# Sliding-window attention into a soft mixture of experts: the first pair of heads loaded as fp32 on another queue, q transposed later in each slot, the mixture's steps a slot later

## The chip, the cores and the metric

The kernel runs on one core of a Trainium2 chip. The core has five engines that work side by side, each with its own instruction queue: TensorE (PE, matmuls; PEld is its weight load), VectorE (DVE), ScalarE (ACT), GpSimd (POOL) and SyncE (SP). DMA transfers are issued from POOL's or SP's queue and run on 16 DMA engines. The metric is the device time of one execution in microseconds (us); lower is better.

## The reference

q, k and v are fp32 of batch 8, heads 8, sequence 576, head size 64. phi is 512 x 32; w1 and w2 hold 8 experts of 512 x 1024 and 1024 x 512.

```
scores = scale * q @ k^T, only where 0 <= row - column < 64
attn   = softmax(scores);  x = attn @ v, laid out as (8*576) x 512
logits = x @ phi
d = softmax of logits over the 4608 rows;  slot_input = d^T @ x   (32 slots, 4 for each expert)
slot_out = relu(slot_input @ w1[e]) @ w2[e]   for each expert
c = softmax of logits over the 32 slots;   out = c @ slot_out
```

## The kernel before

The work is cut into 32 pairs of heads, four pairs to a batch entry. The main loop (L461 to L546) has one slot for each n = 0 to 31, and each slot works on several pairs at different stages. The order of instructions on each engine is the order in which the code is written; each engine takes its queue strictly in turn.

**Loading.** `load_qk` issues from POOL the transfers of q and k for four heads, which turn fp32 into fp16 on the way; `load_v` does it for v and `load_w` for the experts' weights. `join(p)` copies one pair's q and k on POOL into `qi` and `ki`, heads interleaved, for slot p. The first pair's halves are loaded by `load_qk(0, ((0, 2),))`, before anything else on POOL.

**One slot.** PE transposes k (`turn`, into the PSUM tile `kb`) and q (into `qb`); ACT copies them out as `kT` (`keep_k`) and, in two halves, as `qz` (`keep_q`, L258). Scores of the pair three slots back follow: `score_last` into the rest of `kb`, `score_main` into `sc`; `lh` and `rt` add mask and row maximum as a bias. ACT takes the exponentials (`keep_last`, `keep_main`, L308). `st_turn` transposes the attention output x_b of the pair five slots back into the PSUM tile `tx`, and DVE copies it to `xt` (L350). `st_mask` (L265, L266) writes the window mask into the PSUM tile `mx`, on which `st_max` (L275) adds the scores of the pair before; DVE takes the row maximum (`keep_max`, L280). `st_shift` (L284) transposes the maxima, DVE casts them into `rt` (`keep_shift`, L287). `st_av` (L320) multiplies attention by v, `st_norm` normalises on DVE (L329, L330).

**Banks.** `kb`, `qb`, `tx`, the logits `lg` and the slot sums `si` share a ring of two PSUM banks: each new tile takes the bank of the tile before last and waits until that has been read. `mx`, `sc` and `av` are single tiles of their own.

**The mixture's steps.** From n = 8 on, each batch entry's steps are spread over four slots, fi = 0 to 3: the logits (`fr_logits`, `keep_logits`), their running maximum (`fr_max`) and their transposes (`fr_turned`) with the subtraction on POOL (`fr_combine_a`, L405); the exponential (`fr_exp`, L375) and its sums on POOL (`fr_stat`); the transposed dispatch weights (`turn_dispatch`, `keep_dispatch`), the slot sums (`fr_slots`, accumulated on DVE in L446) and the combine weights (`fr_combine_b` on ACT, `fr_combine_c` on DVE, `fr_place` on POOL). After the loop comes a tail: the last pairs, the experts, and the output, which SP's queue writes.

**Constants.** POOL builds the window mask `wb`, the score bias `mb` and `db` (L156 to L170) ahead of the loop; `constants(2)`, in slot 2, copies the bias into `lh` and `rt` on ACT and DVE. DVE's memsets of `kT`, `qz`, `v`'s columns of ones and others precede the loop too.

Of the kernel before, what the change touches and what calls it, by code (L numbers as in the profile page):

```python
# [20 lines left out]
def kernel(  # L21
# [65 lines left out]
    def load_qk(k_, parts=((0, 4),)):  # L87
        b, o = k_ // 2, 4 * (k_ % 2)
        if k_ not in staged:
            staged[k_] = (pin.tile([GP, 4, RQ * Dh], FP16, name="qs", tag="qs"),  # L90
                          pin.tile([GP, 4, RQ * Dh], FP16, name="ks", tag="ks"))
        for h0, h1 in parts:
            for t_, src in reversed(tuple(zip(staged[k_], (q, k)))):
                nc.gpsimd.dma_start(out=t_[:, h0:h1, :],
                                    in_=src[b, o + h0:o + h1].rearrange("h (p r) d -> p h (r d)", r=RQ))
# [34 lines left out]
    load_qk(0, ((0, 2),))  # L130
# [3 lines left out]
    load_qk(0, ((2, 4),))  # L134

# [6 lines left out]
    for t_ in kTs:  # L142
        nc.vector.memset(t_[:, 0:64], 0.0)
    for t_ in qzs:
        nc.vector.memset(t_, 0.0)
# [8 lines left out]
    join(0)  # L154
    load_qk(1)
    mb = ctr[0:64, 96:224]  # L156
    nc.gpsimd.memset(mb, 0.0)
    nc.gpsimd.affine_select(out=mb[:, 0:64], in_=mb[:, 0:64], compare_op=ALU.is_gt,
                            fill=NEG, base=0, pattern=[[1, 64]], channel_multiplier=-1)
    nc.gpsimd.affine_select(out=mb[:, 64:128], in_=mb[:, 64:128], compare_op=ALU.is_ge,  # L160
                            fill=NEG, base=0, pattern=[[-1, 64]], channel_multiplier=1)
    KR = 74
    db = ctr[0:KR, 224:235]
    nc.gpsimd.memset(db[64:KR, :], 0.0)
    nc.gpsimd.affine_select(out=db[64:KR, 0:9], in_=db[64:KR, 0:9], compare_op=ALU.not_equal, fill=-1.0,
                            base=0, pattern=[[-1, 9]], channel_multiplier=1)
    nc.gpsimd.affine_select(out=db[64:KR, 9:10], in_=db[64:KR, 9:10], compare_op=ALU.not_equal, fill=NEG,
                            base=-9, pattern=[[0, 1]], channel_multiplier=1)
    nc.gpsimd.affine_select(out=db[64:KR, 10:11], in_=db[64:KR, 10:11], compare_op=ALU.not_equal, fill=1.0,
                            base=-9, pattern=[[0, 1]], channel_multiplier=1)  # L170

    NR = 2
    ms = [const.tile([128, 33], FP16, name=f"m{i}") for i in range(2)]
    for t_ in ms:
        nc.vector.memset(t_[:, 10:33], 0.0)
    rts = [const.tile([128, 128], FP16, name=f"rt{i}") for i in range(NR)]
# [15 lines left out]
    wm = const.tile([128, 6, 96], FP16, name="wm")  # L192
    for t in range(2):
        nc.vector.tensor_copy(out=wm[64 * t:64 * t + 64],
                              in_=wb[:, :].unsqueeze(1).broadcast_to([64, 6, 96]))
    nc.vector.memset(wm[0:64, 0, 0:64], NEG)
    nc.vector.memset(wm[64:128, 0, 0:32], NEG)
# [8 lines left out]
    def constants(part):  # L206
        if part == 2:
# [28 lines left out]
    for _ in range(2):  # L236
        wp = bank([128, 512], FP32, "wp")
        for _ in range(4):
            nc.tensor.matmul(wp[:, :], warm[:, 0:128], warm[:, :], start=True, stop=True)

    av = pav.tile([128, 2, 512], FP32, name="av", tag="av")
    nc.vector.memset(av[64:128, :, 260:325], 1.0)
    mx = pmx.tile([128, 2, 512], FP32, name="mx", tag="mx")
    nc.vector.memset(mx[:, 1, 384:480], 0.0)

    xbs, pts, xts = {}, {}, {}
# [214 lines left out]
    for n in range(NP):  # L461
        b, hp = divmod(n, HP)
        constants(n)
# [44 lines left out]
        if fi == 3:  # L508
            turn(sides[n][0], qb)
            keep_q(n, qb)  # L510
# [5 lines left out]
        if fi == 1:  # L516
            fr_exp(fb)
        elif fi == 2:
            fr_combine_b(fb)
# [4 lines left out]
        if fi == 0:  # L524
            lg = bank([128, 192], FP32, "lg")
            fr_logits(fb, lg)
            keep_logits(lg, nc.vector.tensor_copy)
        elif fi == 2:
            fr_slots(fb, bank([128, D], FP32, "si"))
        elif fi == 3:  # L530
            fr_place(fb)
        if n >= 1:
            keep_max(n - 1)
        if fi == 0:
            fr_max(fb)
            fr_turned(fb, lgs)
            fr_combine_a(fb)
        elif fi == 1:
            fr_stat(fb)
        elif fi == 2:  # L540
            fr_combine_c(fb)
# [7 lines left out]
    L, M = B - 1, B - 2  # L549

# [263 lines left out]
```

## Time and profile before

| | |
|---|---|
| median of 3 runs | 206.04 us (205.3 to 206.5) |
| the profiled execution | 205.38 us |
| its span, first to last instruction | 203.4 us |
| busy in the span: PE / DVE / ACT / POOL | 156.9 / 137.4 / 137.8 / 121.4 us |
| mean granted TensorE clock | 0.892 of full |
| main loop, from its first transpose to its last mask | 6.0 to 140.9 us |

Times in the rows are microseconds from the span's start. A row of the order of time gives start, duration, engine, line, operation, output tile and input tiles with shapes, how many instructions were merged, and in brackets how long the engine had been idle and what ended that. A duration is that of one instruction with its pipeline, or, for a merged row, from the first start to the last end; instructions of one engine overlap a little, so distances between starts are the better price of one more instruction. A row by stage gives the stretch, its length, busy time (and count) of PE, PEld, DVE, ACT and POOL, the granted clock, the DMA share and GB/s.

### The profile page before, as it was taken

What the parts mean: (1) busy time and instruction counts of PE and PEld (TensorE: products, weight loads), DVE (VectorE), ACT (ScalarE), POOL (GpSimd) and SP (SyncE); (2) the same over time, 40 slices, a digit from 0 to 9 for tenths busy, and PEclk for the clock granted to TensorE, in tenths of its full rate; (3) what the DMA queues carried; (4) which work ended last, traced back from release to release, by engine and by line L of the source; (5) the groups of instructions that cost most, each with busy time, mean ns of one, the idle gap of its engine ahead of it and who ended that gap; (6) DMA issues with size and microseconds to landing.
All of it is one profiled execution on the core that took longest, in us unless ns stands there. A gap on an engine that the chain in (4) does not pass through costs nothing.

```text
span 203.4 us, 6669 instructions
## 1 busy us (share of the span) xinstructions
PE 156.9 (77%) x2832; PEld 112.1 (55%) x2832; DVE 137.4 (68%) x305; ACT 137.8 (68%) x234; POOL 121.4 (60%) x237
## 2 busy tenths in 40 slices
PE   7135988988887988888888788888878899799300
PEld 2124876866765766666767667666663744543000
DVE  6406598887879779687876978778884462299500
ACT  2417799869987977996998797799573132488300
POOL 7999996858994994998699499377500050000000
PEclk9955799999999999999999999999999969855555
DMA  4999999999999999999999999999999920099995
GB/s 57 121 158 186 170 215 196 179 210 200 216 167 220 191 174 225 179 190 199 211 190 182 217 176 191 218 212 216 215 213 216 210 50 0 3 386 412 414 411 236
DMA packets 55725, 40.83 MB, mean 201 GB/s; under 512 B 38672, under 2 KB 50960, under 8 KB 54672
## 3 DMA queue, kind: packets, MB, share of 16 engines
q0 software_dynamic: 53824, 30.97, 108.7%
q1 hardware_dynamic: 1872, 9.44, 11.4%
q8 instruction: 22, 0.36, 0.6%
q14 instruction: 7, 0.06, 0.1%
HBM read 61.93 MB, written 9.44 MB: 351 GB/s over the span
## 4 chain that ended last, share of the span: by engine, by line
PE 39%; DVE 23%; ACT 18%; POOL 7%; issue 5%; DMA 3%; DVEq 0%; POOLq 0%
ACT qz L258 8%; DVE x_b L330 7%; DVE m L280 6%; ACT pt L308 4%; PE qb L251 4%; PE av L320 3%; PE sc L300 3%; PE mx L265 3%; PE sc L303 3%; DMA out_dram<-ob 3%; PE cp L770 3%; PE tx L343 3%; PE hh L715 3%; DVE rt L287 2%; DVE acc L446 2%
## 5 line engine op out<-in xcount | busy, mean ns | idle before, releaser
L258 ACT ACTIVATE qz<-qb 64x576 f16<-64x576 f16 x64 | 52.0, 813 | 2.2 <-PE qb L251 1.8
L280 DVE TENSOR_REDUCE m<-mx 128x10 f16<-128x960 f32 x32 | 36.8, 1151 | 9.3 <-PE mx L275 8.9
L261 ACT ACTIVATE kT<-kb 128x576 f16<-128x576 f16 x32 | 20.8, 651 | 26.3 <-PE kb L292 14.6
L308 ACT ACTIVATE pt<-sc 128x1024 f16<-128x1024 f32 x29 | 29.7, 1025 | 0.9
L330 DVE TENSOR_TENSOR x_b<-av,rc 128x640 f16<-128x640 f32 x32 | 26.4, 824 | 1.1
L251 PE MATMUL kb<-ident_h,ki 96*128 96x96 f16 x192 | 14.4, 214 | 11.7 <-POOL ki L106 11.7
L251 PE MATMUL qb<-ident_h,qi 96*128 96x96 f16 x192 | 14.2, 213 | 7.8 <-DVE lgs L364 4.8
L300 PE MATMUL sc<-rt,lh 128*128 128x128 f16 x248 | 19.2, 221 | 0.9 <-ACT pt L308 0.9
L114 POOL DMA_DIRECT2D vr<-in_v_dram x16 | 19.8, 1239 | 0.2 <-issue 0.2
L251 PEld LDWEIGHTS <-ki 96*128 96x128 f16 x192 | 9.6, 101 | 18.0 <-POOL ki L106 14.1
L350 DVE COPY xt<-tx 128x576 f16<-128x576 f16 x28 | 12.5, 447 | 10.2 <-PE tx L343 10.2
L303 PE MATMUL sc<-qz,kT 128*128 128x128 f16 x248 | 18.9, 219 | 0.0
L275 PE MATMUL mx<-kT,qz 128*64 128x96 f16 x576 | 18.6, 211 | 0.0
L405 POOL TENSOR_TENSOR lgT<-lgT,nm 128x192 f32<-128x192 f32 x7 | 3.5, 504 | 24.1 <-DVE nm L388 24.1
L287 DVE CAST rt<-av 9x128 f16<-9x128 f32 x31 | 9.0, 289 | 12.5 <-PE av L284 11.7
L320 PEld LDWEIGHTS <-pt 128*64 128x64 f16 x576 | 12.7, 110 | 8.4 <-issue 7.3
L251 PEld LDWEIGHTS <-qi 96*128 96x128 f16 x192 | 10.9, 101 | 11.0 <-issue 8.9
L300 PEld LDWEIGHTS <-lh 128*128 128x128 f16 x256 | 16.1, 99 | 1.3 <-issue 1.1
L106 POOL COPY ki<-ks 96x384 int32<-96x384 int32 x32 | 16.1, 502 | 0.9
L320 PE MATMUL av<-vr,pt 128*64 128x65 f16 x288 | 16.1, 197 | 0.0
L106 POOL COPY qi<-qs 96x384 int32<-96x384 int32 x32 | 16.1, 503 | 0.0
L776 DVE TENSOR_SCALAR ob<-cp,rcs 128x512 f32<-128x512 f32 x18 | 13.0, 749 | 4.6 <-PE cp L770 3.1
(183 smaller groups left out, 368.3 us busy)
## 6 DMA issues: line engine op xcount, KB each, us to landing
w<-in_moe_w_dram POOLq DMA_DIRECT2D x15, 1024.0 KB, 14.2
out_dram<-ob SPq DMA_DIRECT2D x11, 768.0 KB, 8.2
vr<-in_v_dram POOLq DMA_DIRECT2D x16, 288.0 KB, 10.3
ks<-in_k_dram POOLq DMA_DIRECT2D x15, 288.0 KB, 9.8
qs<-in_q_dram POOLq DMA_DIRECT2D x15, 288.0 KB, 10.7
w<-in_moe_w_dram POOLq DMA_DIRECT2D x2, 512.0 KB, 20.9
out_dram<-ob SPq DMA_DIRECT2D x1, 512.0 KB, 2.7
ks<-in_k_dram POOLq DMA_DIRECT2D x2, 144.0 KB, 3.8
```

Source lines behind the costliest of these rows:

```text
L106: nc.gpsimd.tensor_copy(out=d_, in_=s_.rearrange("p h r d -> p r h d"))
L114: nc.gpsimd.dma_start(out=vrs[b % 3][:, c0:c1, 0:64], in_=src[:, c0:c1, :])
L251: nc.tensor.transpose(tp[:, j, :], src[:, j].rearrange("p h d -> p (h d)"), ident_h[0:GP, 0:GP])
L258: nc.scalar.activation(dst[r, hl], src[r], AF.Copy, scale=scale)
L261: nc.scalar.activation(kTs[p % NQ][:, 64:64 + S].rearrange("p (g j) -> p g j", j=RQ), ps[:, 0:RQ * GP].rearrange("p (j g) -> p g j", j=RQ) ...
L275: nc.tensor.matmul(mx[64 * t:64 * t + 64, i // 5, 96 * (i % 5):96 * (i % 5) + 96], qz[:, 2 * o:2 * o + 64], kT[:, o:o + 96], start=False, ...
L280: nc.vector.reduce_max(ms[p % 2][:, 0:10].rearrange("p (h c) -> p h c", h=2), mx[:, :, 0:480].rearrange("p h (c x) -> p h c x", x=96), axi ...
L300: nc.tensor.matmul(sc[:, i // 4, 128 * (i % 4):128 * (i % 4) + 128], lh[:, i, :], rts[p % NR][:, :], start=(i % 4 == 0), stop=False, skip_ ...
L303: nc.tensor.matmul(sc[:, i // 4, 128 * (i % 4):128 * (i % 4) + 128], kTs[p % NQ][:, 64 * i:64 * i + 128], qzs[p % NQ][:, 128 * i:128 * i + ...
L308: nc.scalar.activation(pts[p][:, 0:8, :, :], sc[:, :, :].rearrange("p u (c x l) -> p (u c) l x", l=2, x=64), AF.Exp)
L320: nc.tensor.matmul(av[r0:r0 + 64, hl, 65 * (i // 2):65 * (i // 2) + 65], pt[:, i, hl, :], values(b, h, i), start=True, stop=True, skip_gro ...
L330: nc.vector.tensor_tensor(out=x_b[:, :, 128 * hp:128 * hp + 128].rearrange("p c (l d) -> p l c d", l=2), in0=avv[:, :, :, 0:64], in1=rc[:, ...
```

## The change

Three things are changed, and the rest of the diff follows from them.

1. The first pair's q and k are loaded as fp32 from SP's queue, k first, into memory that later holds `x_b` and `xt`; ACT copies q and DVE copies k into the interleaved fp16 form. POOL has one load and one join fewer. POOL's score bias moves from before the loop into slot 1; load 1 moves ahead of it all; in slots 0 and 1 the join comes before the loads, and the load `load_qk(3)` and `load_v(1)` go from slot 0 to slot 1. On DVE the window mask's copies come ahead of most memsets. Six warming matmuls remain of eight.
2. In every slot q is transposed behind scores and mask, and `qz` is copied behind the big exponential. Before, only slots with fi = 3 had that order on PE.
3. The logits come in slot fi = 1 between the turn of k and the scores; maximum and transposes in the same slot; exponential, subtraction and sums in fi = 2, the dispatch weights and slot sums there too; the combine weights in fi = 3; they are placed in the next batch's fi = 0.

```
-    load_qk(0, ((0, 2),))
+    xbs, pts, xts = {}, {}, {}
+    firsts = (pxb.tile([128, 5, D], FP16, name="x_b", tag="x_b"), pxt.tile([128, NKK, S], FP16, name="xt", tag="xt"))
+    firsts = [t_.rearrange("p c d -> p (c d)").bitcast(FP32)[0:GP, 0:2 * RQ * Dh] for t_ in firsts]
+    for t_, src in reversed(tuple(zip(firsts, (q, k)))):
+        nc.sync.dma_start(out=t_.rearrange("p (h e) -> p h e", h=2),
+                          in_=src[0, 0:2].rearrange("h (p r) d -> p h (r d)", r=RQ))
     ident_h = const.tile([128, 128], FP16, name="ident_h")
     make_identity(nc, ident_h)
     load_qk(0, ((2, 4),))
+    load_qk(1)
...
+    sides[0] = (pil.tile([GP, RQ, 2, Dh], FP16, name="qi", tag="qi"),
+                pil.tile([GP, RQ, 2, Dh], FP16, name="ki", tag="ki"))
+    nc.vector.memset(qzs[0], 0.0)
+    nc.vector.memset(kTs[0][:, 0:64], 0.0)
+    for t_, src, eng in zip(sides[0], firsts, (nc.scalar.copy, nc.vector.tensor_copy)):
+        eng(out=t_, in_=src.rearrange("p (h r d) -> p r h d", h=2, r=RQ))
...
-    join(0)
-    load_qk(1)
...
     def constants(part):
-        if part == 2:
+        if part == 1:
+            nc.gpsimd.memset(mb, 0.0)
...
+        elif part == 2:
...
     for n in range(NP):
         b, hp = divmod(n, HP)
-        constants(n)
+        if n + 1 < NP:
+            join(n + 1)
         if n == 0:
             load_v(0)
             load_qk(2)
-        if n + 1 < NP:
-            join(n + 1)
-        if n == 0:
+        elif n == 1:
             load_qk(3)
             load_v(1)
...
+        constants(n)
         load_w(wslot.get(n, 0))
...
         turn(sides[n][1], kb.bitcast(FP16))
-        qb = bank([128, 1024], FP16, "qb")
-        if fi != 3:
-            turn(sides[n][0], qb)
-        if fi == 2:
-            turn_dispatch(qb[:, 640:800])
+        if fi == 1:
+            lg = bank([128, 192], FP32, "lg")
+            fr_logits(fb, lg)
+            keep_logits(lg, nc.vector.tensor_copy)
         if n >= 3:
             score_last(n - 3, kb[:, 384:512])
         keep_k(n, kb.bitcast(FP16))
         if n >= 3:
             keep_last(n - 3, kb[:, 384:512])
-        if fi != 3:
-            keep_q(n, qb)
         if fi == 2:
-            keep_dispatch(fb, qb[:, 640:800])
+            fr_exp(fb)
+            fr_combine_a(fb)
+            fr_stat(fb)
+        elif fi == 3:
+            fr_combine_b(fb)
         if n >= 3:
             sc = psc.tile([128, 2, 512], FP32, name="sc", tag="sc")
             score_main(n - 3, sc)
...
         if n >= 1:
             st_mask()
-        if fi == 3:
-            turn(sides[n][0], qb)
-            keep_q(n, qb)
+        qb = bank([128, 1024], FP16, "qb")
+        if fi == 2:
+            turn_dispatch(qb[:, 640:800])
+        turn(sides[n][0], qb)
+        if fi == 2:
+            keep_dispatch(fb, qb[:, 640:800])
+        keep_q(n, qb)
         if n >= 4:
             st_av(n - 4, av)
...
-        if fi == 0:
-            lg = bank([128, 192], FP32, "lg")
-            fr_logits(fb, lg)
-            keep_logits(lg, nc.vector.tensor_copy)
+        if fi == 1:
+            fr_max(fb)
         elif fi == 2:
             fr_slots(fb, bank([128, D], FP32, "si"))
-        elif fi == 3:
-            fr_place(fb)
+        elif fi == 0 and fb:
+            fr_place(fb - 1)
         if n >= 1:
             keep_max(n - 1)
-        if fi == 0:
-            fr_max(fb)
+        if fi == 1:
             fr_turned(fb, lgs)
-            fr_combine_a(fb)
-        elif fi == 1:
-            fr_stat(fb)
-        elif fi == 2:
+        elif fi == 3:
             fr_combine_c(fb)
```

More of the change, by code (lines that the diff above doesn't have):

```diff
@@ L153 @@
                             base=128, pattern=[[-2, 96]], channel_multiplier=1)
-    join(0)
-    load_qk(1)
     mb = ctr[0:64, 96:224]
[L157 to L161, printed above, removed]
     KR = 74
     db = ctr[0:KR, 224:235]
[L164 to L170, printed above, removed]
-    NR = 2
+    NR = 2
+    wm = const.tile([128, 6, 96], FP16, name="wm")
+    for t in range(2):
+        nc.vector.tensor_copy(out=wm[64 * t:64 * t + 64],
+                              in_=wb[:, :].unsqueeze(1).broadcast_to([64, 6, 96]))
+    nc.vector.memset(wm[0:64, 0, 0:64], NEG)
+    nc.vector.memset(wm[64:128, 0, 0:32], NEG)
+    av = pav.tile([128, 2, 512], FP32, name="av", tag="av")
+    mx = pmx.tile([128, 2, 512], FP32, name="mx", tag="mx")
+    nc.vector.memset(mx[:, 1, 384:480], 0.0)
     ms = [const.tile([128, 33], FP16, name=f"m{i}") for i in range(2)]
@@ L237 @@
         wp = bank([128, 512], FP32, "wp")
-        for _ in range(4):
+        for _ in range(3):
             nc.tensor.matmul(wp[:, :], warm[:, 0:128], warm[:, :], start=True, stop=True)
[L241 to L246, printed above, removed]
     def turn(src, ps):
```

30 lines of the change are left out of this document (16 added, 14 removed).

## The prediction

> **What bounds the kernel now.** I read the chain of waits first, then the busy time by stage, then the order of time in one plain slot, in one batch's four slots and at the start. A slot is one turn of the main loop (n = 0 to 31); batch work (logits, dispatch, slots, combine) begins at n = 8, and fi is the slot's place in its batch. R is the start of the cast at L287, "mask" that of the matmul at L265.
>
> ```profile
> PE 39%; DVE 23%; ACT 18%; POOL 7%; issue 5%; DMA 3%; DVEq 0%; POOLq 0%
> ...
> 78.94:96.20 17.26, 14.70 (x319) 11.63 (x320) 13.75 (x29) 14.60 (x25) 14.35 (x27) 1.00 1.40 194
> ```
>
> No engine owns the chain, and in one batch (17.26 us) PE, DVE, ACT and POOL, in the columns' order less PEld, are busy 14.70, 13.75, 14.60 and 14.35 us. So a slot is set by a loop of waits between engines.
>
> ```profile
> 38.91 0.29 DVE L287 CAST rt<-av 9x128 f16<-9x128 f32 x1 [0.56 <-PE av L284]
> ...
> 40.23 1.15 DVE L280 TENSOR_REDUCE m<-mx 128x10 f16<-128x960 f32 x1
> ...
> 41.43 0.36 PE L265 MATMUL mx<-wm,ident_h 128*128 128x480 f16 x1
> ...
> 42.38 0.29 DVE L287 CAST rt<-av 9x128 f16<-9x128 f32 x1 [0.56 <-PE av L284]
> ```
>
> In a slot without batch work DVE runs from R (38.91) to the end of the row maximum (40.23 + 1.15 = 41.38); the mask matmul has to wait for that, because it overwrites the PSUM tile mx, and starts 0.05 later; from mask to the next R, PE does mask, attention times values and shift, 0.95. Sum 2.47 + 0.05 + 0.95 = 3.47, which is the distance of the two casts. DVE is idle for 0.56 of it. Whatever PE does between mask and shift lengthens the slot; what it does before the mask is free as long as it is done in time.
>
> ```profile
> 79.90 0.34 DVE L368 TENSOR_REDUCE nb<-lgs 128x1 f32<-128x192 f32 x1
> ...
> 80.35 0.37 DVE L383 STREAM_TRANSPOSE lgT<-lgs 128x192 f32<-128x192 f32 x1
> ...
> 80.65 0.37 PE L265 MATMUL mx<-wm,ident_h 128*128 128x480 f16 x1
> ...
> 83.38 0.23 PE L395 MATMUL qb<-ident_h,dd 128*128 128x128 f16 x1 [0.24 <-ACT dd L375]
> ...
> 83.50 0.22 PE L291 MATMUL kb<-rt,lh 128*128 128x128 f16 x1
> ...
> 87.23 0.75 DVE L446 SCALAR_TENSOR_TENSOR acc<-acc,al,si 128x512 f32<-128x512 f32 x1
> ...
> 87.90 1.15 DVE L280 TENSOR_REDUCE m<-mx 128x10 f16<-128x960 f32 x1
> ...
> 89.10 0.36 PE L265 MATMUL mx<-wm,ident_h 128*128 128x480 f16 x1 [0.33 <-DVE m L280]
> ...
> 89.87 1.65 ACT L258 ACTIVATE qz<-qb 64x576 f16<-64x576 f16 x2 [0.31 <-PE qb L251]
> ...
> 90.31 0.29 DVE L287 CAST rt<-av 9x128 f16<-9x128 f32 x1 [0.63 <-PE av L284]
> ...
> 91.56 0.41 PE L251 MATMUL qb<-ident_h,qi 96*128 96x96 f16 x6 [0.56 <-ACT qz L258]
> ...
> 93.27 0.37 PE L265 MATMUL mx<-wm,ident_h 128*128 128x480 f16 x1
> ...
> 94.53 0.51 PE L359 MATMUL lg<-xt,phi_sb 128*32 128x192 f16 x16
> ...
> 94.97 0.43 PE L251 MATMUL kb<-ident_h,ki 96*128 96x96 f16 x6
> ...
> 97.91 0.37 PE L265 MATMUL mx<-wm,ident_h 128*128 128x480 f16 x1
> ```
>
> The batch from mask to mask: fi 0 to 1 to 2 to 3 takes 93.27 to 97.91 = 4.64 for its first step, and 80.65 to 89.10 = 8.45 for the next two; fi 3 to 0 takes 89.10 to 93.27 = 4.17. Sum 17.26, 3.4 over four plain slots of 3.47. The surplus is PE arriving late at the mask: it stands for ACT's exponential before the dispatch transposes (83.38) and for the bank that qz is still being read from (91.56).
>
> **The loop after the change.** Turning q behind the mask puts its six transposes into the loop of waits. The slot fi 3 of before already has that order: mask 89.10 to R 90.31 is 1.21 instead of 0.95. So the plain slot becomes 1.21 + 2.47 + 0.05 = 3.73, 0.26 more, and this holds for every slot in which PE is not late for another reason. Against that stands what no longer makes PE late. Step by step:
> - fi 3 to 0: transposing back (L418) and the copy of lgT run in DVE's idle time; nothing of the batch is on PE, so 3.73 (before 4.17).
> - fi 0 to 1: the logits now come after the turn of k in slot 1. The ring has two banks, and in the new order (kb, tx, qb in slot 0, then kb, lg) lg falls on the bank of slot 0's qb. It waits for both qz copies, which end 89.87 + 1.65 - 89.10 = 2.42 after the mask, 0.04 more to start (91.56). From there to the next mask it was 93.27 - 91.56 = 1.71 with a turn of q in front; the logits take 94.97 - 94.53 = 0.44 where I put 0.25 for the turn, so 1.90. Sum 2.46 + 1.90 = 4.36 (before 4.64).
> - fi 1 to 2: the maximum and running maximum of the logits lie between normalising and the row maximum, 80.35 - 79.90 = 0.45 on DVE: 3.73 + 0.45 = 4.18. ACT used to issue the exponential just ahead of the dispatch transposes that need it; now it is half a slot ahead, and the wait at 83.38 goes. Transpose and maximum of lgT fit DVE's idle time, which has grown by the 0.26.
> - fi 2 to 3: the accumulation adds 87.90 - 87.23 = 0.67 on DVE, the two dispatch transposes, now behind the mask, 83.50 - 83.38 = 0.12: 4.52. Before, the last two steps together took 8.45, now 8.70.
>
> Per batch 3.73 + 4.36 + 4.18 + 4.52 = 16.79 instead of 17.26: 0.47 less. From the mask of n = 8 to that of n = 31 lie five whole batches and the first three steps (13.06 against 13.09): 5 x 0.47 + 0.03 = 2.4 us saved. The placing of the combine weights on POOL a slot later hides in POOL's slack, whose joins now come first in their slot; if POOL had none, it would cost 1 us per batch. ACT's front work (exponentials before the big one of the scores) delays qz, not the mask.
>
> **The start.**
>
> ```profile
> 1.31 0.88 POOL L94 DMA_DIRECT2D ks<-in_k_dram  x1 [0.87 <-POOLq L798]
> ...
> 2.83 0.24 POOL masks.py:197 MEMSET ident_h<- 128x128 f16 x1
> ...
> 5.48 0.49 POOL L106 COPY ki<-ks 96x384 int32<-96x384 int32 x1
> 5.55 1.61 DVE L194 COPY wm<-ctr 64x576 f16<-64x576 f16 x2
> ...
> 6.38 0.68 POOL L94 DMA_DIRECT2D ks<-in_k_dram  x1
> ...
> 7.71 0.22 POOL L157 MEMSET ctr<- 64x128 f16 x1
> ...
> 9.29 2.47 POOL L114 DMA_DIRECT2D vr<-in_v_dram  x2 [0.18 <-issue]
> 11.74 0.70 POOL L94 DMA_DIRECT2D ks<-in_k_dram  x1
> ...
> 13.14 0.50 POOL L106 COPY ki<-ks 96x384 int32<-96x384 int32 x1
> ...
> 15.36 2.44 POOL L114 DMA_DIRECT2D vr<-in_v_dram  x2
> 16.36 1.16 DVE L280 TENSOR_REDUCE m<-mx 128x10 f16<-128x960 f32 x1 [8.48 <-PE mx L275]
> 17.44 0.73 DVE L209 COPY lh<-ctr 64x1152 f16<-64x1152 f16 x1
> 17.79 0.52 POOL L106 COPY ki<-ks 96x384 int32<-96x384 int32 x1
> 19.79 0.22 DVE L214 TENSOR_TENSOR lh<-lh,ctr 10x64 f16<-10x64 f16 x1
> 21.10 1.16 DVE L280 TENSOR_REDUCE m<-mx 128x10 f16<-128x960 f32 x1 [0.43 <-PE mx L275]
> 24.42 1.16 DVE L280 TENSOR_REDUCE m<-mx 128x10 f16<-128x960 f32 x1
> ...
> 20.00:22.00 2.00, 2.00 (x33) 1.84 (x33) 1.20 (x3) 1.21 (x2) 1.96 (x4) 0.50 1.44 191
> 22.00:24.00 2.00, 2.00 (x32) 1.70 (x31) 0.25 (x1) 1.61 (x4) 1.90 (x5) 0.79 2.40 158
> ...
> qs<-in_q_dram POOLq DMA_DIRECT2D x2, 144.0 KB, 3.9
> ```
>
> POOL works without a gap from 1.31 to 17.79; pair 1 is joined only at 13.14, behind two loads, and DVE idles 8.48 us for it. The change takes from POOL the first pair's two issues (2.83 - 1.31 = 1.52) and one join (6.38 - 5.48 = 0.90), 2.42 us, and moves its constants (9.29 - 7.71 less 0.18 idle = 1.40) behind the second load of v. That move has a price: the score bias that DVE and ACT copy in slot 2 comes from them, and everything of that slot is queued behind those copies on both engines, so the earlier first pairs bring nothing by themselves. POOL by rows: identity, second pair's issue and window mask (2.65), then load 1 (1.33), end near 5.5; the second pair's q half, issued by 2.8, lands 3.9 later, and its join ends at 7.2. Then v 2.45, load 2 1.40, join and load 3 2.22 (13.14 to 15.36), v 2.43, constants 1.40: end 17.1, the first half at 16.4. DVE's copies and the last addition took 17.44 to 20.01 = 2.57; from 16.4 they end at 19.0, the cast ends at 19.3, and the row maximum of slot 2 ends at 20.45 instead of 22.26: 1.8 earlier. PE takes part of it back. It had half the clock up to 22, though busy all of 20 to 22, and slot 3 now runs earlier than that with an idle PE behind it. Its score matmuls (some 0.9, below) and the 1.21 from mask to R can take up to 2.1 longer at half clock; DVE's own work covers more than half of that, and I take 0.8. So the row maximum at 24.42 comes 1.0 earlier. Slots 4 and 5 keep it (constants on DVE cover the 0.26 there), slots 6 to 8 pay 0.26 each. At n = 8 about 0.2 is left; bounds are 1.8 - 0.8 = 1.0 gained and, if the join waits for a loaded queue, a loss (second rival).
>
> The fp32 loads go to SyncE's queue, which issues nothing until the outputs, and the two copies of the first pair to ACT and DVE, which have nothing else then: no cost while POOL's 17.1 is what slot 2 waits for, about 1 us if not. The memsets moved behind lie in the 8.48. At the end, the transposed weights are placed after the last weight issues, and qz of n = 31 ends about 0.1 later behind the big exponential: 0.1 lost.
>
> **A page's rule against the change.** DVE's copy of the k half is the one large fp32 copy from SBUF to SBUF, and it runs while POOL issues load 1. If such a copy held POOL up, POOL's chain would be longer by the copy, and with it every number behind 17.1. The rows speak against it only weakly: POOL's issue at 6.38 beside DVE's copies of 5.55 took 0.68, the one at 11.74 with DVE idle 0.70; but those copies are fp16 and broadcast. DVE's copies there take 1.61 / 2 = 0.8 for 576 elements, so I price the case at 0.8: 204.3. The Trainium skill, page "SBUF — State Buffer", section on the three doors, says that an fp32 copy on VectorE locks GpSimd out of the port it writes descriptors through, for the whole instruction; no row of before has such a copy.
>
> **Sum.** 2.4 (loop) + 0.2 (start) - 0.1 (end) = 2.5. The profiled execution took 205.38 us with a span of 203.4; it becomes 202.9 with a span of 200.9. That execution lies 0.66 under the median of the runs, 206.04, so the median becomes 203.5.
>
> **Rivals.**
> - Slower: ACT's qz as the new bound. tx of the next slot takes the bank of this slot's qb, so PE waits at tx if qz ends too late. It ends 2.42 after the mask when ACT starts it at once; PE, ready 1.90 after the mask (91.56 less its 0.56 idle), reaches tx after the score matmuls, which are most of the 1.71 that follow, say 0.9: at 2.8. The margin is 0.4. The big exponential now stands ahead of qz, and in fi 2 and 3 further exponentials ahead of that. If qz came 0.8 late in these two slots, each would lose 0.4, 12 x 0.4 = 4.8 us: 208.3. It turns from gain to loss at 0.2 beyond the margin. For: ACT is busy 14.60 of 17.26. Against: at 16.79 it still has 2.2 idle.
> - POOL stands at the first join. The second pair's halves now travel beside two fp32 transfers twice as large in SBUF. If they land at 6.3 instead of 3.9, all of it goes into POOL's chain: 203.5 + 2.4 = 205.9. For: twice the bytes in flight. Against: nothing else is in flight then.
> - The loads hold the loop at 17.26: the gain of 2.4 goes, 205.9. For: 194 GB/s with DMA above 1.0 in that batch. Against: PE waited for no load there.
>
> **Chances.** The forecast 0.50, own range 202.0 to 205.0; ACT's qz 0.15; first join 0.20; loads 0.10; the lock-out 0.05. The range reaches from 202.0 (the start keeping its 1.0 and the loop 0.1 a batch more than summed) to 207.2, which takes in the two cases at 205.9 and leaves out most of the slow one. A measurement of this kernel can tell about 0.5%, 1.0 us. Below 205.0: nearly all of the forecast and the lock-out, a little of the join, 0.56; above 207.1: qz and the late end of the join, 0.20; between, 0.24.
>
> **What would show it.** Right: mask to R 1.21 in plain slots, slots of 3.73 at n = 6 and 7; a batch of 16.8 with steps 4.36, 4.18, 4.52, 3.73; PE idle before lg put down to qz; no POOL wait for nm; POOL's constants ending near 17 and the row maximum of pair 2 near 23.4. Wrong: PE waiting for qz before tx; POOL idle before the first join beyond 7; a batch of 17.2 or more; a start whose slot 8 comes later than 41.4.

## The result, and the profile after

The changed kernel takes 204.05 us (median of 20 runs) where the kernel before, run beside it, takes 205.82 (20 runs): ratio 0.9905, interval 0.988 to 0.993, 1.8 us by the medians. The prediction was 203.5, from 206.04. Some executions of a kernel are a per cent or more slower than its others; the ratios leave these out, the medians don't.

The rows of after come from the second profiled execution of the changed kernel, which took 204.04 us with a span of 201.9. The first one took 206.12 with a span of 204.0. Of these 2.1 us, 0.9 lie in the tail, where the granted clock fell earlier, and 1.2 in the start: its mask of n = 8 stood at 42.87, not at 41.67, most of that by one slot, in which DVE's cast of L235 took 1.18 instead of 0.37 beside copies of POOL's. So a single profile's start is not a sharp measure; the section on the hardware comes back to that. The change moves the code by eight lines: the mask is L273, the cast R is L295, the row maximum L288, the running maximum of the logits L377 (L369 before).

The chain of waits, and by stage two batches (columns as in the prediction: PE, PEld, DVE, ACT, POOL, clock, DMA share, GB/s):

```profile
PE 43%; DVE 26%; ACT 11%; issue 6%; POOL 5%; DMA 4%; DVEq 0%; POOLq 0%; ACTq 0%
```

```profile
75.28:92.05 16.77, 14.27 (x319) 11.98 (x319) 13.65 (x29) 14.57 (x26) 14.42 (x27) 1.00 1.44 202
92.05:109.23 17.18, 14.10 (x319) 11.96 (x319) 14.05 (x29) 14.72 (x26) 13.85 (x26) 1.00 1.46 195
```

The chain is still shared among the engines. The batch of 17.26 became 16.77, and the next one is 17.18, nearly as before. Busy time by itself doesn't tell what lies between them, except that DVE has 0.40 more. The order of time does:

```profile
75.28 0.36 PE L273 MATMUL mx<-wm,ident_h 128*128 128x480 f16 x1 [0.53 <-DVE m L288]
...
75.59 0.42 PE L259 MATMUL qb<-ident_h,qi 96*128 96x96 f16 x6
...
76.05 1.64 ACT L266 ACTIVATE qz<-qb 64x576 f16<-64x576 f16 x2 [0.31 <-PE qb L259]
76.49 0.29 DVE L295 CAST rt<-av 9x128 f16<-9x128 f32 x1 [0.63 <-PE av L292]
...
77.74 0.51 PE L367 MATMUL lg<-xt,phi_sb 128*32 128x192 f16 x16 [0.55 <-ACT qz L266]
...
79.65 0.37 PE L273 MATMUL mx<-wm,ident_h 128*128 128x480 f16 x1
...
82.56 0.16 DVE L377 TENSOR_TENSOR run<-run,nb 128x1 f32<-128x1 f32 x1
82.63 1.15 DVE L288 TENSOR_REDUCE m<-mx 128x10 f16<-128x960 f32 x1
82.91 0.67 POOL L119 COPY vs<-vr 64x576 int32<-64x576 int32 x1
...
83.83 0.36 PE L273 MATMUL mx<-wm,ident_h 128*128 128x480 f16 x1 [0.42 <-DVE m L288]
...
88.33 0.36 PE L273 MATMUL mx<-wm,ident_h 128*128 128x480 f16 x1
...
92.05 0.36 PE L273 MATMUL mx<-wm,ident_h 128*128 128x480 f16 x1 [0.53 <-DVE m L288]
...
96.42 0.37 PE L273 MATMUL mx<-wm,ident_h 128*128 128x480 f16 x1
...
99.17 0.66 POOL L119 COPY vs<-vr 64x576 int32<-64x576 int32 x1
99.33 0.52 DVE L377 TENSOR_TENSOR run<-run,nb 128x1 f32<-128x1 f32 x1
99.77 1.15 DVE L288 TENSOR_REDUCE m<-mx 128x10 f16<-128x960 f32 x1
...
100.96 0.36 PE L273 MATMUL mx<-wm,ident_h 128*128 128x480 f16 x1 [1.34 <-DVE m L288]
```

Mask to mask, the batch that starts at 75.28 has the steps 4.37, 4.18, 4.50 and 3.72; the next has 4.37, then 96.42 to 100.96 = 4.54. In that slot DVE's running maximum, a single column of 128 x 1, takes 0.52 instead of 0.16. It starts at 99.33, when POOL's copy of v has run since 99.17, and it ends (99.85) when that copy ends (99.83). Everything behind it on DVE, the row maximum above all, comes later, and the next mask with it. POOL's copy at 82.91 came behind the running maximum, and cost nothing. The last two batches are like the one at 99.33: 0.62 and 0.48, ending with a copy of POOL's to 0.01. In the first three it takes 0.16.

The start:

```profile
3.72 0.69 POOL L94 DMA_DIRECT2D qs<-in_q_dram  x1
4.11 0.69 DVE L153 CAST ki<-xt 96x768 f16<-96x768 f32 x1 [2.00 <-DMA xt<-in_k_dram]
4.38 0.53 POOL L157 MEMSET ctr<- 64x96 f16 x1
...
5.61 0.64 DVE L169 COPY wm<-ctr 64x576 f16<-64x576 f16 x2 [0.80 <-POOL ctr L160]
...
6.60 0.50 POOL L106 COPY ki<-ks 96x384 int32<-96x384 int32 x1 [1.03 <-DMA ks<-in_k_dram]
...
7.52 0.50 POOL L106 COPY qi<-qs 96x384 int32<-96x384 int32 x1 [0.42 <-DMA qs<-in_q_dram]
...
17.20 0.74 DVE L223 COPY lh<-ctr 64x1152 f16<-64x1152 f16 x1 [5.71 <-POOL ctr L212]
...
17.68 0.18 POOL L219 TENSOR_SCALAR_AFFINE_SELECT ctr<-ctr 10x1 f16<-10x1 f16 x1
...
20.14 1.16 DVE L288 TENSOR_REDUCE m<-mx 128x10 f16<-128x960 f32 x1
...
22.03 0.61 PE L273 MATMUL mx<-wm,ident_h 128*128 128x480 f16 x1
...
24.31 1.16 DVE L288 TENSOR_REDUCE m<-mx 128x10 f16<-128x960 f32 x1 [0.43 <-PE mx L283]
```

The row maximum of slot 2 starts at 20.14 (before 21.10), that of slot 3 at 24.31 (before 24.42). POOL's constants end at 17.86. The mask matmul of slot 3 takes 0.61 where others take 0.36: PE is at half speed there (granted clock 0.50 from 20 to 24).

Where the time went, by three places that can be read in any of the profiles (us; the tail is the span less the mask of n = 31):

| kernel | mask of n = 8 | mask of n = 31 | loop between | tail | span |
|---|---|---|---|---|---|
| before | 41.43 | 140.88 | 99.45 | 62.5 | 203.4 |
| changed | 41.67 | 139.83 | 98.16 | 62.1 | 201.9 |
| start alone | 41.70 | 141.55 | 99.85 | 63.0 | 204.5 |
| loop alone | 41.75 | 139.51 | 97.76 | 63.3 | 202.8 |
| q ahead | 40.98 | 135.35 | 94.37 | 62.0 | 197.4 |
| logits behind | 41.13 | 138.60 | 97.47 | 63.1 | 201.7 |
| bias early | 40.26 | 137.93 | 97.67 | 62.1 | 200.0 |
| warmed | 40.34 | 138.74 | 98.40 | 62.4 | 201.1 |
| shift behind | 41.86 | 139.92 | 98.06 | 62.1 | 202.0 |
| q ahead, bias early | 40.43 | 134.89 | 94.46 | 60.8 | 195.7 |

So in these profiles the change loses 0.24 in the start and gains 1.29 in the loop; 0.4 more come in the tail.

### The profile page after: what moved, and what is told of

Same layout as the page of the kernel before. It is cut to its first block, busy times and chain, and to the rows that moved or that the text cites. A ratio compares the mean times of both kernels' runs of the same rounds, so it can differ in the third digit from the quotient of the medians.

```text
span 204.0 us, 6686 instructions
## 1 busy us (share of the span) xinstructions
PE 154.6 (76%) x2830; PEld 115.7 (57%) x2830; DVE 138.4 (68%) x306; ACT 139.1 (68%) x235; POOL 120.4 (59%) x233
## 4 chain that ended last, share of the span: by engine, by line
PE 41%; DVE 25%; ACT 13%; DMA 8%; issue 5%; POOL 3%; DVEq 0%; POOLq 0%; ACTq 0%
ACT qz L266 9%; DVE m L288 8%; DVE x_b L338 6%; PE mx L273 4%; DMA qs<-in_q_dram 4%; DMA out_dram<-ob 4%; PE qb L259 4%; PE sc L311 3%; PE sc L308 3%; PE hh L719 3%; PE av L328 3%; PE tx L351 3%; PE cp L774 3%; DVE rt L295 2%; PE ops L742 2%
## 5 line engine op out<-in xcount | busy, mean ns | idle before, releaser
L288 DVE TENSOR_REDUCE m<-mx 128x10 f16<-128x960 f32 x32 | 36.8, 1149 | 0.6 <-PE mx L283 0.4
L295 DVE CAST rt<-av 9x128 f16<-9x128 f32 x31 | 9.0, 289 | 18.1 <-PE av L292 17.9
L259 PEld LDWEIGHTS <-ki 96*128 96x128 f16 x192 | 10.2, 100 | 17.9 <-POOL ki L106 8.7
L283 PE MATMUL mx<-kT,qz 128*64 128x96 f16 x576 | 19.4, 213 | 0.7 <-issue 0.7
L273 PE MATMUL mx<-wm,ident_h 128*128 128x480 f16 x32 | 12.1, 378 | 9.7 <-DVE m L288 8.9
L311 PE MATMUL sc<-qz,kT 128*128 128x128 f16 x248 | 19.4, 222 | 0.0
L283 PEld LDWEIGHTS <-qz 128*64 128x64 f16 x576 | 16.2, 115 | 1.0 <-issue 0.8
L311 PEld LDWEIGHTS <-kT 128*128 128x128 f16 x256 | 16.0, 99 | 0.0
```

Of the source, the lines that this page charges most:

```text
L259: nc.tensor.transpose(tp[:, j, :], src[:, j].rearrange("p h d -> p (h d)"), ident_h[0:GP, 0:GP])
L273: nc.tensor.matmul(mx[:, 0, 0:480], ident_h[:, :], wm[:, 0:5, :], start=True, stop=False, skip_group_check=True)
L283: nc.tensor.matmul(mx[64 * t:64 * t + 64, i // 5, 96 * (i % 5):96 * (i % 5) + 96], qz[:, 2 * o:2 * o + 64], kT[:, o:o + 96], start=False, ...
L288: nc.vector.reduce_max(ms[p % 2][:, 0:10].rearrange("p (h c) -> p h c", h=2), mx[:, :, 0:480].rearrange("p h (c x) -> p h c x", x=96), axi ...
L311: nc.tensor.matmul(sc[:, i // 4, 128 * (i % 4):128 * (i % 4) + 128], kTs[p % NQ][:, 64 * i:64 * i + 128], qzs[p % NQ][:, 128 * i:128 * i + ...
```

## The experiments

My theory after the result was: the loop carries the gain, by taking the batch's steps out of PE's way to the mask; the start gains nothing; and q's turn between mask and shift gives most of the loop's gain back, 0.26 in every slot. The rivals: the start carries it; or q's turn behind the mask is itself what brings the gain, by letting the batch's steps go ahead.

**The changed kernel once more**, beside the next three, which share its chip and its runs of before.

> The changed kernel once more, for another profile. All theories: 1.8 us faster than the kernel before. Steps from mask to mask in a batch 4.37, 4.19, 4.49, 3.72. The first profile had the mask of n = 8 at 42.87 (before 41.43) and the weight matmuls of the tail at a lower clock; if these belong to that execution, the mask of n = 8 comes near 41.5 here; if the start is really slower, again near 42.9.

204.36 us (10 runs), ratio 0.9941 (0.991 to 0.9971). Its profile is the one read above.

**The start alone.** The changed kernel with the loop's batch steps and q's place as before:

```
-        if fi == 1:
-            lg = bank([128, 192], FP32, "lg")
...
+        qb = bank([128, 1024], FP16, "qb")
+        if fi != 3:
+            turn(sides[n][0], qb)
...
+        if fi == 0:
+            lg = bank([128, 192], FP32, "lg")
...
-        elif fi == 0 and fb:
-            fr_place(fb - 1)
+        elif fi == 3:
+            fr_place(fb)
```

> The start alone (fp32 loads, constants and joins moved), the loop as before. My theory: the start brings nothing by itself, 0 to 1 us either way against before (the mask of n = 8 between 40.5 and 42.5), and the batch stays at 17.26. Rival, the start carries the gain: 1.5 us faster or more.

206.5 us, ratio 1.0043 (1.0016 to 1.007): slower by 0.9. The mask of n = 8 comes at 41.70 although slots 6 and 7 cost only 3.47 here, and the batch takes 17.26 to 17.33 as before, but for one of 17.62.

**The loop alone.** The kernel before, with the loop's body of the changed kernel, and the last weights placed behind the loop.

> The loop alone (q turned behind the scores, the mixture's steps a slot later), the start as before. My theory: a batch of 16.8 instead of 17.26, 2.0 to 2.8 us off between n = 8 and n = 31, up to 1 us lost in the slots 4 to 8, so 1.2 to 2.2 us faster than before. Rival, the gain is the start's: 0.5 us slower to the same.

204.48 us, ratio 0.9912 (0.9873 to 0.9951). The loop between takes 97.76, 1.69 less than before. By the ratios the two parts add up, +0.9 and -1.8 against -1.2 together, but the intervals are wide: one execution of 201.87 carries part of the -1.8, and by the medians of all runs it is 1.0. What is sure is the side: the loop carries the gain; that the start carries it is out.

**q ahead.** The changed kernel with q's turn and the dispatch transposes ahead of the mask; the batch's steps stay where the change put them:

```
-        if n >= 1:
-            st_mask()
         qb = bank([128, 1024], FP16, "qb")
...
         keep_q(n, qb)
+        if n >= 1:
+            st_mask()
         if n >= 4:
             st_av(n - 4, av)
```

> The changed kernel with the turn of q and of the dispatch weights put ahead of the mask, ACT's order left as changed. My theory, the turn behind the mask lies in the loop of waits: plain slot 3.47 instead of 3.73, and wherever PE is not late (three steps of four) 0.26 to 0.38 less, so 5 to 6 us faster than the changed kernel if ACT keeps up, 3 us if ACT's 14 us a batch begins to bind. Rival, ACT or the two-bank ring sets the slot already: no change within 1 us.

199.25 us, ratio 0.9686 (0.9645 to 0.9727): 5.1 under the changed kernel beside it. The plain slots in its order of time:

```profile
34.04 0.36 PE L273 MATMUL mx<-wm,ident_h 128*128 128x480 f16 x1 [0.35 <-DVE m L288]
34.99 0.29 DVE L295 CAST rt<-av 9x128 f16<-9x128 f32 x1 [0.64 <-PE av L292]
...
37.51 0.36 PE L273 MATMUL mx<-wm,ident_h 128*128 128x480 f16 x1 [0.27 <-DVE m L288]
```

Mask to R is 0.95 again, the slot 3.47, and PE still waits for DVE at the mask: q's turn fits in front of it. So two parts of the change work against each other. This kernel is about 6 us faster than the one before, 5.1 of it in the loop (99.45 to 94.37); moving q behind the mask takes 3.8 of these 5.1 away again. That the batch's steps need q behind the mask is out. The 5.1 belong to the steps' new places together with q's: here too q is turned behind the scores, and `qz` copied behind the big exponential. The steps with q where it was before weren't tried.

**The logits behind the scores.** fi 0 to 1 is 4.37 because PE waits for qz ahead of lg (the row at 77.74). Here the logits come behind the scores in slot 1, where qz has long been read:

```
-        if fi == 1:
-            lg = bank([128, 192], FP32, "lg")
-            fr_logits(fb, lg)
-            keep_logits(lg, nc.vector.tensor_copy)
         if n >= 3:
             score_last(n - 3, kb[:, 384:512])
...
             score_main(n - 3, sc)
             keep_main(n - 3, sc)
+        if fi == 1:
+            lg = bank([128, 192], FP32, "lg")
+            fr_logits(fb, lg)
+            keep_logits(lg, nc.vector.tensor_copy)
```

> The changed kernel with the logits put behind the main scores instead of ahead of them. My theory, PE waits at lg for both qz copies because lg takes their bank: behind the scores PE comes to lg later than that wait ends, the step fi 0 to 1 falls from 4.37 to 3.73 to 3.9, six times 0.5 to 0.6, so 3 to 3.8 us faster than the changed kernel. Rival, the step is long because 0.44 of logits are added on PE wherever they stand: 0 to 1 us.

203.88 us, ratio 0.9894 (0.9821 to 0.9967), against 0.9941 and 0.9905 for the changed kernel: not the 3 to 3.8 us expected, but the rival's 0 to 1, though not for its reason, since the step did fall. (The intervals of this and the next three kernels overlap the changed kernel's 0.988 to 0.993: their runs alone price none of these edits, and the marks in the profiles have to.) fi 0 to 1 fell to 3.72 to 3.74 in all six batches, and the next two steps took it back: fi 1 to 2 is 4.39 to 4.83, and fi 2 to 3 4.43 to 5.34. In the order of time:

```profile
44.72 0.52 DVE L372 COPY lgs<-lg 128x128 f32<-128x128 f32 x2
44.86 0.36 PE L273 MATMUL mx<-wm,ident_h 128*128 128x480 f16 x1
...
45.39 0.41 PE L259 MATMUL qb<-ident_h,qi 96*128 96x96 f16 x6
...
46.29 0.29 DVE L295 CAST rt<-av 9x128 f16<-9x128 f32 x1 [0.55 <-PE av L292]
```

In the ring the bank of lg is the one that qb takes next. The copies out of lg now end at 45.24, behind the mask, and q's turn follows at 45.39, 0.53 behind the mask (0.31 at 75.59 of the changed kernel, where nothing holds it); R comes 1.43 behind the mask, not 1.21. So the bank's wait moved from in front of lg to the place behind the mask, where it is paid in full, and part of the gain went there. Why fi 2 to 3 is longer wasn't settled.

**The bias early.** POOL makes the score bias ahead of the first load of v:

```
         if n == 0:
+            constants(1)
             load_v(0)
...
-        constants(n)
+        if n != 1:
+            constants(n)
```

> The changed kernel with POOL's score bias built in slot 0, ahead of the loads of v, instead of in slot 1. My theory, the constants at the end of POOL's chain hold slot 2's copies on ACT and DVE: kT of slot 2 no longer waits (before the edit it starts near 18.9), the mask of slot 3 comes 1.0 to 1.5 earlier than 22.0, and 0.7 to 1.5 us are gained in all. Rival, PE's clock or the third join (near 18 either way) sets slot 3: 0 to 0.4 us.

203.36 us, ratio 0.9843 (0.9778 to 0.9908).

```profile
16.11 1.16 DVE L288 TENSOR_REDUCE m<-mx 128x10 f16<-128x960 f32 x1 [0.43 <-PE mx L283]
...
18.06 0.66 PE L259 MATMUL kb<-ident_h,ki 96*128 96x96 f16 x6 [1.99 <-POOL ki L106]
...
20.44 0.60 PE L273 MATMUL mx<-wm,ident_h 128*128 128x480 f16 x1
```

The row maximum of slot 2 comes at 16.11 instead of 20.14, 4 us earlier; that of slot 3 (22.71) only 1.6, and the mask of n = 8 1.4 earlier (0.9 to 2.6, against the four profiles of the changed start named below). Slot 3 now waits for its own pair's join (1.99 at 18.06), behind the second load of v, and PE is still at half speed; but what slot 2 stood for were the constants behind the loads.

**Warmed.** Nine matmuls on zeros into the scores' tile behind slot 2, which nobody reads, so that PE has work while slot 3 waits for the constants.

> The changed kernel with nine 512-column matmuls behind slot 2 on PE, whose result is not used, so that PE does not idle before slot 3. Theory, the half clock takes back what the start had gained: granted clock 1.0 from about 19 on, slot 3 about 1 us shorter, the row maximum of slot 3 (24.4) near 23.3, 0.5 to 1.0 us faster in all. Rival, POOL's chain sets slots 3 and 4: no change within 0.3 us.

203.34 us, ratio 0.9852 (0.9786 to 0.9917). In the order of time, slot 3:

```profile
21.41 0.36 PE L273 MATMUL mx<-wm,ident_h 128*128 128x480 f16 x1
...
22.72 1.16 DVE L288 TENSOR_REDUCE m<-mx 128x10 f16<-128x960 f32 x1
```

The mask matmul takes 0.36 where the changed kernel's took 0.61. With slot 2's row maximum at 20.20, as in the changed kernel, slot 3's starts at 22.72 instead of 24.31: half speed costs 1.6 there, and the mask of n = 8 comes 1.3 earlier (0.8 to 2.5 against the four).

**The shift behind.** POOL's copy of v in the slots fi = 2 behind the subtraction and the sums of the batch:

```
-        if hp in (2, 3):
-            shift_v(b, hp - 2)
+        if hp == 3:
+            shift_v(b, 1)
...
             fr_combine_b(fb)
+        if hp == 2:
+            shift_v(b, 0)
```

> The changed kernel with POOL's shifting of v in the slots fi 2 put behind its subtraction and sums. Theory, the step fi 1 to 2 is 4.5 instead of 4.19 in the batches in which DVE's small sum of two SBUF operands (the running maximum) meets that copy on POOL and takes 0.52 instead of 0.16: now 0.16 and 4.19 in all six, 0.9 to 1.2 us faster. Rival, those steps are long for another reason (ACT's exponentials, joins): they stay at 4.5 in the later batches, no gain.

202.63 us, ratio 0.9823 (0.9757 to 0.9888). The running maximum takes 0.16 in all batches (mean over its seven 159 ns; in the changed kernel 323), and fi 1 to 2 is 4.18 or 4.19 in five batches of six. So the long running maximum is POOL's copy, and without it five of the six steps are as predicted. The profiled execution (203.79, above the median) shows no net gain in the loop, for other steps between n = 14 and 20 are longer, among them this one:

```profile
82.96 0.16 DVE L377 TENSOR_TENSOR run<-run,nb 128x1 f32<-128x1 f32 x1
...
83.36 0.23 PE L299 MATMUL kb<-rt,lh 128*128 128x128 f16 x1 [1.39 <-DVE run L377]
```

PE stands 1.39 in front of the scores' bias. The running maximum, to which the wait is put down, is nothing that this matmul reads. Such stops of PE, some put down to no engine, are in other kernels' profiles too (1.06 in front of the same matmul with q ahead); their cause stays open.

**Versions put together.** q ahead with the bias early; the same with two more edits (DVE's constants of slots 4 and 5 in slot 1, the shift behind); and, with the logits behind too, without and with the shift behind.

> The changed kernel with two edits at once: q's turn and the dispatch transposes go back ahead of the mask (alone 199.25 us, 5 to 6 us under the changed kernel), and POOL's score bias goes ahead of the loads of v (alone mask of n = 8 at 40.26 instead of 41.67). Theory: the two places are independent, the start being what slots 2 and 3 wait for and the loop a ring of waits, so the gains add: mask of n = 8 near 39.6 (40.98 less 1.4), the same steps as with q ahead alone, 199.25 - 1.4 = 197.8 us. Rival: at the start the one gain eats the other, since slots 6 and 7 are already at 3.47 and the loads of v now stand behind the bias: 199 us or more.

198.42 us, ratio 0.965 (0.9561 to 0.9739): the fastest, not measurably apart from q ahead alone (0.9686). The mask of n = 8 came 0.55 earlier than there, not 1.4, so the rival was nearer.

> As the kernel with q ahead and the bias early, with two more edits: DVE's constants of slots 4 and 5 are made in slot 1, where DVE waits, and POOL's shift of v in the slots fi = 2 stands behind the subtraction and the sums. Theory: the running maximum of fi = 1 is then 0.16 in every batch, not 0.5 (with the plain slot at 3.47 a step fi 1 to 2 of 3.92), and slots 4 and 5 are short of the constants' time on DVE, some 0.5 each: 196 to 197.5 us. Rival: POOL's copy, put behind, holds up another row of DVE or PE, as the longer steps of n = 14 to 20 with the shift behind alone may have been: 197.8 us or more, and fi 2 to 3 or 3 to 0 longer by what fi 1 to 2 gains.

201.81 us, ratio 0.9739 (0.9638 to 0.984): no gain, as the rival had it. The theory had nothing to win on the running maximum: in the fastest version it already takes 0.16 in all six batches.

> The changed kernel with q ahead, the bias early, DVE's constants of slots 4 and 5 in slot 1, and the logits behind the scores, with POOL's shift of v where it was. Theory: with the logits behind, the wait for both qz copies ahead of lg is off PE's path in fi 0 to 1 (alone it fell from 4.37 to 3.73), so that step is 3.5; but the copies of the logits come later on DVE, and with the logits behind alone the next two steps gave most of it back. Carried over: 196 to 198 us. Rival: with q ahead the ring gives lg another bank, lg waits for nothing, and putting the logits behind only makes the steps fi 1 to 2 and 2 to 3 longer: 198 us or more, slower than q ahead with the early bias.

201.96 us, ratio 0.98 (0.9722 to 0.9878).

> As the one before (q ahead, bias and constants early, logits behind), with POOL's shift of v in the slots fi = 2 behind the subtraction and the sums. Theory: the running maximum takes 0.16 in each batch instead of 0.5 to 0.6 in the later ones; it lies on DVE between normalising and the row maximum, so about 0.35 each in four or five batches: 1 to 1.7 us less than without this edit, 194.5 to 196.5 us. Rival: with the logits behind, DVE comes to the running maximum after POOL's copy has ended, so nothing is gained: within 0.5 us of the one before.

200.33 us, ratio 0.9709 (0.9595 to 0.9822): 1.6 under the version without the shift behind. That is the size that the theory gave for the edit, but the intervals overlap, and the profiles don't show its mechanism: without the edit the running maximum is long in one batch of six, by 0.13 (0.29), with it in two, by 0.08 and 0.17, beside a join. So the agreement is chance, or has another cause. All four versions stayed above the level that their theories gave, the first by 0.6, the others by some 4.

What bounds these versions can be looked for in the fastest one. Its chain of waits:

```profile
DMA 32%; POOL 19%; PE 18%; ACT 14%; issue 7%; DVE 4%; DVEq 0%; POOLq 0%; ACTq 0%
```

PE's groups between the masks of n = 8 and n = 31, the idle time before them last; first the mask of the changed kernel, then three of the fastest version:

```profile
L273 PE MATMUL mx<-wm,ident_h 128*128 128x480 f16 x23 | 8.4, 364 | 8.3 <-DVE m L288 8.1
```

```profile
L259 PE MATMUL kb<-ident_h,ki 96*128 96x96 f16 x138 | 10.0, 207 | 4.2 <-ACT qz L266 3.2 <-issue 0.7 <-DVE rc L337 0.2
L273 PE MATMUL mx<-wm,ident_h 128*128 128x480 f16 x23 | 8.4, 365 | 0.0
L367 PE MATMUL lg<-xt,phi_sb 128*32 128x192 f16 x96 | 3.1, 247 | 2.9 <-ACT qz L266 2.9
```

And its order of time on POOL and ACT, at the two longest stops of POOL behind a load:

```profile
35.91 0.68 POOL L94 DMA_DIRECT2D qs<-in_q_dram  x1 [2.86 <-DMA w<-in_moe_w_dram]
...
97.27 0.69 POOL L94 DMA_DIRECT2D ks<-in_k_dram  x1 [2.63 <-DMA w<-in_moe_w_dram]
...
100.99 0.50 POOL L413 TENSOR_TENSOR lgT<-lgT,nm 128x192 f32<-128x192 f32 x1
...
101.53 0.36 ACT L419 ACTIVATE lgs<-lgT 128x192 f16<-128x192 f32 x1 [1.14 <-POOL lgT L413]
```

In the changed kernel's loop PE stands 8.1 us for DVE at the mask. In the fastest version that wait is gone, and PE stands for ACT: 6.1 us for `qz`, in front of a turn of k and of the logits, and 2.4 for the exponential in front of the dispatch transposes. The chain runs through the loads, but where they cost PE time are single steps. POOL stands 2.9 us at the issue of a load, its next join comes later, and PE waits 0.65 for `ki` in slot n = 7; in the changed kernel that stop is 1.34, and no wait of PE follows. In the version with two more edits PE waits 2.26 there and the slot takes 5.36; in the one with the logits behind it takes 6.83 (a wait of 2.36, and a granted clock of 0.70 from 36 to 41). The stops at 97.27 (2.63) and 98.82 (0.85) make POOL's subtraction late, ACT waits 1.14 for it ahead of the big exponential, and the step from the mask at 100.88 to that at 105.46 takes 4.58 instead of 3.47. So the rival that "the loads hold the loop" was wrong of this change, and in the faster versions is right of single steps, not of the whole loop.

## Why the prediction was right, point by point

- **The plain slot** 3.73, mask to R 1.21: measured 3.72 to 3.73 and 1.20 to 1.21. Right, and q ahead shows its price: 0.26 a slot would be 6 us over 23 slots; measured 3.8, since without it other waits set some of the slots.
- **fi 0 to 1** 4.36 by a wait for qz ahead of lg: 4.36 or 4.37 in all six batches, the wait 0.55 where the trace puts it. **fi 2 to 3** 4.52: 4.44 to 4.55. **fi 3 to 0** 3.73: 3.72 or 3.73.
- **fi 1 to 2** 4.18: right in two batches (4.19, 4.18), 4.31 in the first, and 4.54, 4.65, 4.51 in the last three. This is the term that was mis-sized: I took 0.45 for maximum and running maximum together from a place where no copy of POOL's ran, and moved the pair to one in which POOL, already at the next slot's work, copies v, without asking what DVE's two operands would meet there. The loop saved 1.29 instead of 2.44, 1.15 less, and the last three batches hold all of it: 0.36 + 0.47 + 0.33 = 1.16. (In the first batch the running maximum is short; its 0.13 has another cause, and is balanced by fi 2 to 3, on the whole 0.17 shorter than summed.)
- **PE's stops before.** My list of what made PE late left out the longest one of each batch, below: q's turn waited 0.8 for the bank from which DVE was still copying the logits. The sum didn't suffer, as the new steps were summed afresh, but the wait is gone in the new order, and may be part of why moving the steps pays.

```profile
78.94 0.42 PE L251 MATMUL qb<-ident_h,qi 96*128 96x96 f16 x6 [0.81 <-DVE lgs L364]
```

- **The start** +0.2: measured -0.24. The failed step is POOL's chain. Its constants end at 17.86 where I summed 17.1: the second pair's halves took longer to land (POOL waits 1.03 and 0.42 for them, and the first join ends near 8.0 instead of 7.2). So slot 2's row maximum came 0.96 earlier than before, not 1.8. From there to the next row maximum the half speed took 0.85 more than before (24.31 less 20.14, against 24.42 less 21.10), where I had 0.8, and 0.1 was left. The slots up to the mask of n = 8 then cost 0.35, where I had summed three times 0.26: slots 7 and 8 paid 0.51, slots 5 and 6 0.32, but slot 4 gave 0.49 back. POOL's chain is short of the sum in all four profiles that have this start (constants ending at 17.86 to 18.05); the -0.24 is one of them, the mask of n = 8 standing at 41.13 to 42.87.
- **The end** -0.1: the tail is 0.4 shorter in this profile. Tails differ by up to 2.4 with the clock: in the second 15 us of the tail the granted clock is 0.77 in those of 63.0 to 63.3, 0.89 in those of 62.0 to 62.5, 1.00 in that of 60.8. So nothing can be read from this.
- **The sum:** 0.44 from the start and 1.15 from the loop were missed, some 0.5 came from the tail: a span of 201.9 against 200.9. That half us was not forecast; it is luck, and so is part of how near the forecast came.

By its own signs the forecast was right in part: the slots and three of the four steps came as written. POOL's constants and the row maximum of pair 2 did not (17.86 and 24.31, not near 17 and 23.4), and three signs that were to show it wrong came. Two batches took 17.19 and 17.23, POOL was idle before the first join until 7.52, and slot 8 came at 41.67. POOL also waited for nm, 1.2 to 1.9 in the last three batches, without a cost that the steps show.

The rivals. ACT's qz as the bound: PE waited for it nowhere in front of tx. It shows in front of lg, as summed, and in front of the turn of k in the slots fi = 3 (3.1 in all), which I hadn't summed and which lengthened no step. The first join: real, at a third of its price, 0.8 of 2.4. The median transfer of the second pair's k half took longer:

```profile
ks<-in_k_dram POOLq DMA_DIRECT2D x1, 144.0 KB, 5.0
```

That is 5.0 us beside the fp32 transfers, where the halves of before took 3.8 and 3.9; whether these transfers are the reason wasn't tried apart. The lock-out: DVE's fp32 copy ran from 4.11 to 4.80, and POOL's memset, started within it, took 0.53 and ended at 4.91, where before it took

```profile
4.67 0.20 POOL L149 MEMSET ctr<- 64x96 f16 x1
```

0.20. So POOL was held, for 0.3, and not for the copy's whole length: the last issue of load 1 had begun 0.39 before the copy (3.72, with 0.69 as long as the issues beside no copy), and the memset came when 0.42 of the copy were left. In eleven of the twelve profiles with this copy the memset takes 0.52 to 0.56. In the twelfth, the shift behind, the copy came earlier, 0.15 behind the start of the issue, and it is the issue that is held, 0.94 instead of 0.68 to 0.70, while the memset behind it takes 0.20:

```profile
3.71 0.94 POOL L94 DMA_DIRECT2D qs<-in_q_dram  x1
...
3.86 0.56 DVE L153 CAST ki<-xt 96x768 f16<-96x768 f32 x1 [1.76 <-DMA xt<-in_k_dram]
```

So this rival is real at a third of its 0.8. It cost nothing here, as POOL then stood 0.6 to 1.4 for its load in all twelve.

The running maximum is the same thing the other way round, and here too a page had the rule: the Trainium skill, "SBUF — State Buffer", section "Who interferes with whom", says that a VectorE instruction with two SBUF inputs and a GpSimd instruction that reads SBUF exclude each other, the second one waiting for the first to end. The rows agree: it ends with POOL's copy in each long case, and costs nothing where DVE is first. I had weighed that page only for the copy. The joins on POOL do the same where they meet it (0.42 once with q ahead).

## What to carry to other kernels

Ask of every step that is moved not only what it costs, but what runs beside it at the new place: a 0.16 us instruction became 0.5 because it met another engine's copy. Split a change with several parts: here the steps' new places, with q behind the scores, were worth 5 us in the loop, and turning q behind the mask as well gave 3.8 back in steps of 0.26. When PE waits for DVE at the mask, work ahead of the mask is free and work behind it is paid in full, until PE waits for something else.

## What the runs showed of the hardware

- The granted clock isn't always what PE ran at. In the kernel with the bias early it reads 1.00 in the stage in which slot 3's mask matmul (at 20.44, above) takes 0.60, as long as at a granted 0.50 in the changed kernel (0.61). Of the twelve profiles with the new start ten have 0.57 to 0.61 there, the warmed one 0.36, and one other 0.37. At the start a matmul's own duration is the better witness.

```profile
20.00:22.00 2.00, 2.00 (x25) 1.54 (x24) 0.01 (x1) 1.25 (x2) 1.85 (x4) 1.00 1.69 190
```

- When the full speed comes back varies for the same code. The two versions with the logits behind have the same instructions in the same order up to n = 8; slot 3's mask matmul took 0.37 at 20.98 in one and 0.60 at 21.11 in the other, and the mask of n = 4 followed at 23.91 and 25.00. The two profiles of the changed kernel, the logits behind and the shift behind are alike in this way too: their masks of n = 4 stand at 25.86, 26.11, 24.93 and 26.32, those of n = 8 at 42.87, 41.67, 41.13 and 41.86. The Trainium skill, "TensorE: Matmul & The Clock Gate", section "What's actually happening", says that the window by which the gate opens runs freely, so that the same kernel meets it at a different phase; that fits the masks of n = 4. By the marks at n = 8, where other waits add to it (DVE's cast of 1.18 in the first), a start can't be compared by one profile to better than 1.7.
- The two copies of the window mask on DVE took 0.64 together where POOL stood waiting for its load; before, beside two copies of POOL's and an issue, 1.61.
